# A decode layer's forward and backward pass: dP rows turned by VectorE, dq four heads at a time, rows spread by one product, P of pairs by two groups, wq as 32-bit words

## The chip, the cores and the metric

The kernel runs on one core of a Trainium2 chip, in one launch. The metric is the time of one execution on the device in microseconds (us); the time before is the median of three runs. Engines are named as in the profile: PE is TensorE, DVE VectorE, ACT ScalarE, POOL GpSimd, and SP the engine whose queue issues nearly all DMA transfers, in order.

## The reference, cut to what matters

One decode step (one query row per batch element) of a pre-layernorm attention block with a cached K and V, followed by a gated MLP, and the gradients with respect to all inputs. B = 4, H = 32 heads (128 batch-heads in all), 4096 cached positions, head size 128, width 512, F = 1792, all bfloat16.

```python
def _A_ref(x, k_cache, v_cache, wq, wo):
    q = (x @ wq).reshape(B, Sq, H, Dh) ...
    scores = jnp.einsum("bhqd,bhkd->bhqk", q, k_cache) * (Dh ** -0.5)
    p = _softmax(scores, axis=-1)
    o = jnp.einsum("bhqk,bhkd->bhqd", p, v_cache)
    return (...o...).reshape(B, Sq, H * Dh) @ wo
x = A_x
h = x + _A_ref(_layernorm(x), A_k_cache, A_v_cache, A_wq, A_wo)
h2 = h + _B_ref(_layernorm(h), B_w1, B_w3, B_w2)
...
_out, _vjp = jax.vjp(_f, A_x, A_k_cache, A_v_cache, A_wq, A_wo, B_w1, B_w3, B_w2)
_grads = _vjp(grad_out)
```

For each batch-head, with one query row, the gradient of V is the outer product of P (4096) and dO (128), and the gradient of K the outer product of dS (4096) and q (128). dS = P * (dP - c), with dP = V dO and c = sum(P * dP). K and V are 1 MB for each batch-head (128 MB each), and so are their gradients: 128 MB of K read once, 128 MB of V read twice, and two gradients of 128 MB written.

## The kernel before, in words

The kernel is built with an explicit order: instructions stand on each engine in the order in which the Python code calls them. Semaphore waits are put in where a tile or a slot is reused.

SBUF holds an arena of 23 slots of 1 MB (`Slot`; two neighbours make a `Slot2`). In the first part of the gradient stage a slot is taken from the head of a list of free slots (`free`), and `give`/`gave` appends it at the end. Taking a slot is decided when the program is built. Whoever writes into it at run time waits until its last users are done: PE for a V slot, the landing of the store for a gradient slot.

The work goes in four stages.
1. Up to about 655 us: for each batch-head, K is transposed, scores, softmax and P are computed, and M = V^T (P K), a 128x128 matrix, is kept in f32 (it holds o, and dq is computed from it). The weights are loaded at the end of it.
2. The middle, to about 700 us: attention output, layernorm, MLP forward and backward, and dh. At its end the first two dV products (`grad_V(0)`, `grad_V(1)`) are made, whose slots are kept in `first_gv`, and V of batch-heads 0 to 8 has been asked for (`load_V2`).
3. Batch-heads 0 to 31 one by one (`SP = 32`): `front(s)` transposes V as 32-bit words (four groups: PE transposes, ACT copies back, `words_T`, L792 to L799) and multiplies it by dO. Eight matmuls (L1245) add a head's dP into one PSUM tile of four heads, through the windows `zd` that POOL fills (`dO_window`, L1211). Then the V slot is given back (L1249 to L1253). `rows_out` (ACT, L1221) and `rows_T` (PE, L1228) turn the rows, `group_dS` (DVE, L1261, L1264) makes dS for four heads. `grad_V(s)` and `grad_K(s)` make the outer products on DVE (`outer`, L813) and store them (L824, L1271). P is doubled for `outer` by POOL (`P_pairs`, L1216); the rows of dO and q are spread to all partitions four heads at a time by `replicate` (PE, L1186, ACT, L1189).
4. Batch-heads 32 to 127 as 48 pairs, 2 MB each: `front_pair`, `group_dS_pair`, `grad_pair` (products L1400, stores L1410), `P_rows` and `replicate_pair` do the same for two heads.

Beside stages 3 and 4 run three generators, a step at a time (`side`): "o" (the rest of dO; `dO_rows`), "q" (`dq_work`: one matmul by M for each batch-head, L1007) and, from s = 35, "s" (dx, the weights' gradients and the second output).

The order in which stage 3 begins is the caller's loop (L = 5, `more_V` calls `grad_V`):

```python
for s in range(L):
    load_ahead(s)
    front(s)
    if s == 0:
        for gv in first_gv:
            gv.give()
    more_V((4, 6, 7, 8, 9)[s])
```

`load_ahead` issues the next V load once `front` has put a V slot into `vring`. A V slot goes there only when fewer than seven V slots are held; the first two go to `free`.

Of the kernel before, what the change touches and what calls it, by code (L numbers as in the profile page):

```python
# [21 lines left out]
SP = 32  # L22
# [5 lines left out]
def kernel(  # L28
# [133 lines left out]
    rows_t = pers.tile([32 + B, D], FP32, name="rows_t")  # L162
# [638 lines left out]
    def words_of(v, g, k):  # L801
        return v.rearrange("p (x r t) -> p t x r", r=Dh, t=2)[:, k, 4 * g:4 * g + 4]
# [40 lines left out]
    with ExitStack() as cm:  # L843
# [77 lines left out]
        dh = rs.f(2080)[0:B, 1024:1024 + D]  # L921
# [50 lines left out]
    with ExitStack() as c2:  # L972
        psT = c2.enter_context(tc.tile_pool(name="psT2", bufs=2, space=bass.MemoryType.PSUM))
        psD = c2.enter_context(tc.tile_pool(name="psD", bufs=1, space=bass.MemoryType.PSUM))
# [29 lines left out]

        def dq_work():
            for s in range(NH):
                nc.tensor.matmul(dq_ps[:, s:s + 1], lhsT=M_of(s)[:, 0:Dh], rhs=dOT_f[:, s:s + 1], start=True, stop=True)  # L1007
                if s % MC == MC - 1:
                    Ms[s // MC].give()
                    if s // MC in (5, 6):  # L1010
                        load_wq2(s // MC - 5)
                if s % 4 == 3:
                    yield
# [3 lines left out]
        def side_work():  # L1017
# [4 lines left out]
            t = rs.f(2080)[:, 1536:1536 + NH]  # L1022
            nc.vector.tensor_tensor(out=t, in0=c_rep[:], in1=kPT[:], op=ALU.mult)
            nc.vector.tensor_tensor(out=t, in0=dq_ps[:, 0:NH], in1=t, op=ALU.subtract)
# [6 lines left out]
            nc.scalar.copy(out=dqr_bf[:], in_=pt[:])  # L1031
            flat = Slot("dqflat")
# [7 lines left out]
            for cc in range(DC):  # L1040
                wq2 = wq2s.popleft()
                wv = wq2.b(HD).rearrange("p (n c) -> p n c", c=P)
                for h0 in range(0, H, 8):
                    pt = psg.tile([P, 8, P], BF16, tag="gps", name="pt_wq")
                    for i in range(8):
                        nc.tensor.transpose(pt[:, i, :], wv[:, h0 + i, :], ident_b[:])
                    yield
                    nc.scalar.copy(out=wv[:, h0:h0 + 8, :], in_=pt[:])
                yield
                for h in range(H):  # L1050
                    nc.tensor.matmul(dx_ps[0:B, cc * P:(cc + 1) * P], lhsT=dqT_bf[:, h * B:(h + 1) * B], rhs=wv[:, h, :],
                                     start=(h == 0), stop=(h == H - 1))
                    if h == H // 2 - 1:
                        yield
                wq2.give()
                load_wq2(cc + 2)
                yield
# [10 lines left out]
            nc.vector.tensor_tensor(out=dx_bf, in0=dh, in1=lnbx, op=ALU.add)  # L1068
# [22 lines left out]
            nc.gpsimd.tensor_copy(out=dh_bf, in_=dh)  # L1091
# [71 lines left out]
        def rest_of_dO():  # L1163
            for pg in range(1, H // 8):
# [6 lines left out]
                mid_w["wo"][pg].give()  # L1171
                yield
# [5 lines left out]
        units["o"] = rest_of_dO()  # L1178
        def replicate(nm_, i0):
# [3 lines left out]
            rows = dOrows_bf if nm_ == "rdo" else qrows_bf  # L1183
            ps = psrep.tile([P, REP, Dh], FP32, tag="rep", name="rep_ps")
            for i in range(REP):
                nc.tensor.matmul(ps[:, i, :], lhsT=ident_b[0:K_, i0 + i:i0 + i + 1].to_broadcast([K_, P]), rhs=rows[0:K_, :],  # L1186
                                 start=True, stop=True)
# [7 lines left out]
        dOw = bw3.tile([P, 2, SP], BF16, name="dOw", tag="dOw", bufs=1)  # L1195
        for i in range(B):
            nc.gpsimd.memset(zd[i][:], 0.0)
# [20 lines left out]
        def rows_out():  # L1218
            if "ps" in rows:
                rows["sb"] = bw3.tile([P, 512], FP32, tag="dPr", name="dPr", bufs=1)  # L1220
                nc.scalar.copy(out=rows["sb"][:], in_=rows.pop("ps")[:])  # L1221

        def rows_T():
            if "sb" in rows:
                sb = rows["t"] = rows.pop("sb")
                rows["T"] = psD.tile([P, B, P], FP32, tag="dPT", name="dPT_ps")
                for jj in range(4):
                    nc.tensor.transpose(rows["T"][:, jj, :], sb[:, jj * P:(jj + 1) * P], ident_f[:])  # L1228

        def front(s):  # L1230
            hl = s % B
            if s not in VTs:
                for g in range(SJ // GW):
                    V_T(s, psT, range(g, g + 1))
                    if hl == 0 and g == 0:
                        rows_out()
                    if hl == 0 and g == 2:
                        rows_T()
            v = VTs[s].t[:, 0:SJ * Dh]
            if hl == 0:  # L1240
                rows["acc"] = psD.tile([P, 512], FP32, tag="dP", name="dP_ps")
            dO_window(s + 2)
            for k in range(2):
                for c in range(4):
                    nc.tensor.matmul(rows["acc"][32 * c:32 * (c + 1), :], lhsT=zd[hl][:, k, :], rhs=words_of(v, c, k),  # L1245
                                     start=(hl == 0 and k == 0), stop=(hl == B - 1 and k == 1), tile_position=(0, 32 * c))
            if hl == B - 1:
                rows["ps"] = rows.pop("acc")
            sl = VTs.pop(s)  # L1249
            if nv["next"] < SP and len(V2s) + len(VTs) + len(vring) < NV2:  # L1250
# [296 lines left out]
```

## Time and profile before

| what | value |
|---|---|
| time, median of 3 runs | 1688.53 us (1688.17 to 1689.38) |
| the profiled execution's own time | 1688.41 us |
| its span, first to last instruction | 1686.6 us |
| PE / DVE / ACT / POOL busy | 75% / 73% / 57% / 23% of the span |
| bytes moved by DMA | 707.21 MB, mean 419 GB/s |
| mean granted PE clock | 0.855 |
| largest waits | DVE L1400 for the landing of stores, 260.1 us; POOL L453 for ACT, 409.5 us; SP's queue for DVE L1400, 559.8 us |

A busy share is a mean over stages. The page cuts the span into 40 slices of 42 us: a digit is the busy share of a slice in tenths, and the GB/s row is what the transfers moved. A line of a group or of the timeline has the line of the code, the engine, the operation, what it writes and reads with shapes, and in brackets how long the engine stood idle before it and what ended that. A wait is put down to the last of several semaphores.

### The profile page before, as it was taken

What the parts mean: (1) busy time and instruction counts of PE and PEld (TensorE: products, weight loads), DVE (VectorE), ACT (ScalarE), POOL (GpSimd) and SP (SyncE); (2) the same over time, 40 slices, a digit from 0 to 9 for tenths busy, and PEclk for the clock granted to TensorE, in tenths of its full rate; (3) what the DMA queues carried; (4) which work ended last, traced back from release to release, by engine and by line L of the source; (5) the groups of instructions that cost most, each with busy time, mean ns of one, the idle gap of its engine ahead of it and who ended that gap; (6) DMA issues with size and microseconds to landing.
All of it is one profiled execution on the core that took longest, in us unless ns stands there. A gap on an engine that the chain in (4) does not pass through costs nothing.

```text
span 1686.6 us, 33967 instructions
## 1 busy us (share of the span) xinstructions
PE 1260.6 (75%) x14188; PEld 924.3 (55%) x14188; DVE 1233.9 (73%) x1198; ACT 960.9 (57%) x1492; POOL 379.6 (23%) x663
## 2 busy tenths in 40 slices
PE   5989888888888888878878666667766677776660
PEld 4777777677667766745555544544434444444440
DVE  5999899989998997667766476576565656555673
ACT  3455454445445454677666556666655676666650
POOL 1221222222232222234541131111120101011020
PEclk9999999999999999799899778777678676567775
DMA  9999999999999999999999999999999999999996
GB/s 400 424 424 424 425 423 425 424 424 421 418 423 411 424 411 397 398 410 426 425 426 428 429 429 429 431 430 429 429 430 430 429 429 431 430 429 431 430 429 259
DMA packets 80986, 707.21 MB, mean 419 GB/s; under 512 B 8748, under 2 KB 12984, under 8 KB 15296
## 3 DMA queue, kind: packets, MB, share of 16 engines
q1 hardware_dynamic: 80416, 704.94, 99.2%
q8 instruction: 112, 1.84, 0.4%
q14 instruction: 42, 0.34, 0.0%
q0 software_dynamic: 416, 0.10, 0.0%
HBM read 422.59 MB, written 282.34 MB: 418 GB/s over the span
## 4 chain that ended last, share of the span: by engine, by line
DMA 35%; DVE 7%; ACT 5%; PE 5%; issue 3%; DVEq 0%; SPq 0%; POOL 0%; ACTq 0%
DMA out_dram<-arena 34%; DVE arena L1400 7%; ACT arena L799 5%; PE pt_tps L798 1%; PE dq_ps L1007 1%; PE dP_ps L1245 1%; DMA arena<-in_A_v_cache_dram 1%; PE pt_wo L610 0%; DVEq L1542 0%; PE rep_ps L1186 0%; DVE dPr L1342 0%; ACT dPr L1221 0%; PE dOT_ps L773 0%; PE dPT_ps L1228 0%; PE c_ps L784 0%
## 5 line engine op out<-in xcount | busy, mean ns | idle before, releaser
L799 ACT COPY arena<-pt_tps 128x1024 bf16<-128x1024 bf16 x512 | 491.7, 1023 | 249.0 <-PE pt_tps L798 247.3
L798 PE MATMUL pt_tps<-ident_f,arena 128*128 128x128 f32 x2048 | 410.7, 356 | 202.9 <-DMA arena<-in_A_v_cache_dram 125.6
L798 PEld LDWEIGHTS pt_tps<-ident_f,arena 128*128 128x128 f32 x2048 | 304.1, 182 | 349.3 <-issue 191.6
L1400 DVE TENSOR_TENSOR arena<-arena 128x8192 bf16<-128x8192 bf16 x48 | 212.5, 4427 | 197.9 <-DMA out_dram<-arena 192.5
L457 DVE TENSOR_TENSOR arena<-arena 128x4096 bf16<-128x4096 bf16 x128 | 292.4, 2285 | 24.0 <-POOL arena L453 24.0
L472 PE MATMUL M_ps<-arena 128*128 128x130 bf16 x4096 | 286.9, 223 | 30.0 <-DMA arena<-in_A_v_cache_dram 29.2
L472 PEld LDWEIGHTS <-arena 128*128 128x128 bf16 x4096 | 254.6, 99 | 49.6 <-DMA arena<-in_A_v_cache_dram 42.5
L1400 DVE TENSOR_TENSOR arena<-dS,arena 128x8192 bf16<-128x8192 bf16 x48 | 212.3, 4424 | 67.6 <-DMA out_dram<-arena 67.6
L364 DVE STREAM_TRANSPOSE arena<-arena 128x512 f32<-128x512 f32 (+1 forms) x321 | 250.6, 797 | 0.0
L359 ACT COPY arena<-pt_tps 128x1024 bf16<-128x1024 bf16 x128 | 129.4, 1012 | 180.4 <-PE pt_tps L358 149.6
L1397 POOL COPY arena<-arena 128x128 bf16<-128x128 bf16 x48 | 43.7, 912 | 432.7 <-ACT arena L1374 200.0
L370 POOL TENSOR_TENSOR W<-qrep,wmask 128x128 bf16<-128x128 bf16 x128 | 120.8, 944 | 85.4 <-PE S_ps L390 70.6
L453 POOL COPY arena<-P_all 128x64 bf16<-128x64 bf16 x128 | 32.7, 256 | 412.5 <-ACT P_all L447 409.5
L1308 POOL COPY arena<-arena 64x4 bf16<-64x4 bf16 x96 | 68.8, 717 | 136.3 <-PE dP_ps L1328 108.6
L1328 PE MATMUL dP_ps<-arena 128*32 128x512 bf16 x768 | 84.4, 471 | 8.4 <-ACT arena L799 8.3
L813 DVE TENSOR_TENSOR arena<-dS,arena 128x4096 bf16<-128x4096 bf16 x32 | 73.1, 2291 | 21.8 <-DMA out_dram<-arena 21.5
L447 ACT COPY P_all<-pt_P 32x64 bf16<-32x64 bf16 x256 | 52.1, 203 | 54.1 <-PE pt_P L443 51.8
L358 PE MATMUL pt_tps<-ident_b,arena 128*128 128x128 bf16 x1024 | 80.8, 224 | 0.0
L482 PE MATMUL kP_ps<-arena,onesw 128*32 128x512 bf16 x1024 | 79.4, 387 | 0.0
L813 DVE TENSOR_TENSOR arena<-P,arena 128x4096 bf16<-128x4096 bf16 x29 | 66.3, 2291 | 17.7 <-DMA out_dram<-arena 17.5
L422 ACT ACTIVATE E<-S_ps,nm 128x256 f32<-128x256 f32 x64 | 30.4, 474 | 82.7 <-DVE nm L419 82.6
L991 PE MATMUL gps<-arena 4*128 4x512 bf16 x110 | 47.3, 452 | 39.0 <-ACT arena L985 39.0
(246 smaller groups left out, 1494.7 us busy)
## 6 DMA issues: line engine op xcount, KB each, us to landing
out_dram<-arena SPq DMA_DIRECT2D x96, 2048.0 KB, 27.4
arena<-in_A_v_cache_dram SPq DMA_DIRECT2D x160, 1024.0 KB, 15.6
arena<-in_A_k_cache_dram SPq DMA_DIRECT2D x128, 1024.0 KB, 15.4
arena<-in_A_v_cache_dram SPq DMA_DIRECT2D x48, 2048.0 KB, 31.7
out_dram<-arena SPq DMA_DIRECT2D x72, 1024.0 KB, 19.8
arena<-in_A_wq_dram SPq DMA_DIRECT2D x8, 1024.0 KB, 14.3
arena<-in_B_w_dram SPq DMA_DIRECT2D x8, 896.0 KB, 15.0
out_dram<-arena SPq DMA_DIRECT2D x6, 896.0 KB, 27.6
```

Of the source, the lines that this page charges most:

```text
L358: nc.tensor.transpose(pt[:, i, :], Kn[:, c * GW + i, :], ident_b[:])
L359: nc.scalar.copy(out=KT[:, c * GW:(c + 1) * GW, :], in_=pt[:])
L364: nc.vector.transpose(out=KT[:, c * w_:(c + n) * w_], in_=Kn[:, c * w_:(c + n) * w_])
L370: nc.gpsimd.tensor_tensor(out=W[:, hl], in0=qrep[:, :, s:s + 1].to_broadcast([P, 4, 32]), in1=wmask[:, hl, None, :].to_broadcast([P, 4, 32 ...
L457: nc.vector.tensor_tensor(out=PK[:, :, 0:Dh].rearrange("p j (r t) -> p j r t", t=2), in0=Ks[s].heads().rearrange("p j (r t) -> p j r t", t=2),
L472: nc.tensor.matmul(hold["M"][:], lhsT=Vn[:, j, :], rhs=PK[:, j, :], start=(j == 0), stop=(j == SJ - 1))
L482: nc.tensor.matmul(hold["kP"][32 * q:32 * (q + 1), :, :], lhsT=ones_window(w), rhs=PK[:, j0:j0 + 4, 0:Dh], start=(w == 0 and c == 0), stop ...
L798: nc.tensor.transpose(ptw[:, jj, :], w[:, 4 * g + jj, :], ident_f[:])
L799: nc.scalar.copy(out=v.rearrange("p (j d) -> p j d", d=Dh)[:, g * GW:(g + 1) * GW, :], in_=pt[:])
L813: nc.vector.tensor_tensor(out=dst.rearrange("p j (r t) -> p j r t", t=2), in0=col2[:, :, None, :].to_broadcast([P, SJ, Dh // 2, 2]), in1=r ...
L1328: nc.tensor.matmul(rows["acc"][32 * c:32 * (c + 1), :], lhsT=zt[t % B][:, k, ZP - m:ZP - m + 32], rhs=words_of(v, 2 * c + u, k), start=(pl ...
L1400: nc.vector.tensor_tensor(out=dst.rearrange("p (j r t) -> p j r t", r=Dh // 2, t=2), in0=col2[:, :, None, :].to_broadcast([P, 2 * SJ, Dh / ...
```

## The change

Six parts, by what they do:
- The dP rows of a group, in PSUM, are turned by one VectorE transpose of 32x32 blocks (`rows_turned`) in place of a ScalarE copy and four PE transposes. `words_of` takes other columns so that the blocks land where they are wanted, and the windows of the pairs (`zt`) are laid out anew.
- `front` no longer multiplies at its end: it puts the head into `pend`, and `products()` makes its matmuls and gives the slot back, in the middle of the next `front` (at g = 2), or after `side` in the main loop.
- dq is computed for four heads by one f32 matmul of 512 columns against a window of four dO columns (`dz`, filled by POOL); the wanted diagonal is taken out at the end of the generator (`m4f`) and turned once.
- Rows of dO and q are spread by one POOL product each (`spread`, with a mask `m4`), so that `replicate` is one matmul of 512 columns in place of four of 128; `replicate_pair` likewise two in place of eight.
- P of pairs (`P_rows`) is made for two groups by four matmuls.
- wq is transposed as 32-bit words: 64 f32 transposes in place of 128, with dq's words split to match (`dqw`). `dh` moves to `rows_t`.

```diff
-        dh = rs.f(2080)[0:B, 1024:1024 + D]
+        dh = rows_t[64:64 + B, :]
+        RM = {nm_: rs.t[:, 2048 + 512 * k:2560 + 512 * k].rearrange("p (i d) -> p i d", i=REP) for k, nm_ in enumerate(("rq", "rdo"))}
...
-        psD = c2.enter_context(tc.tile_pool(name="psD", bufs=1, space=bass.MemoryType.PSUM))
+        psD = c2.enter_context(tc.tile_pool(name="psD", bufs=2, space=bass.MemoryType.PSUM))
...
+        dz = rs.t[:, 4032:4152].bitcast(FP32)
+        nc.gpsimd.memset(dz, 0.0)
+
         def dq_work():
-            for s in range(NH):
-                nc.tensor.matmul(dq_ps[:, s:s + 1], lhsT=M_of(s)[:, 0:Dh], rhs=dOT_f[:, s:s + 1], start=True, stop=True)
-                if s % MC == MC - 1:
+            for s in range(0, NH, 4):
+                nc.gpsimd.tensor_copy(out=dz[:, 28:32], in_=dOT_f[:, s:s + 4])
+                yield
+                g, c = s % 32 // 4, s // 32
+                Mv = Ms[s // MC].f(MC * (Dh + 1)).rearrange("p (n c) -> p n c", c=Dh + 1)[:, s % MC:s % MC + 4, 0:Dh]
+                nc.tensor.matmul(dq_ps[32 * c:32 * (c + 1), :], lhsT=dz[:, 28 - 4 * g:60 - 4 * g], rhs=Mv, start=(g == 0), stop=(g == 7),
+                                 tile_position=(0, 32 * c))
+                if s % MC == MC - 4:
                     Ms[s // MC].give()
                     if s // MC in (5, 6):
                         load_wq2(s // MC - 5)
-                if s % 4 == 3:
-                    yield
+            yield
 
...
-                    pt = psg.tile([P, 8, P], BF16, tag="gps", name="pt_wq")
-                    for i in range(8):
-                        nc.tensor.transpose(pt[:, i, :], wv[:, h0 + i, :], ident_b[:])
+                    pt = psg.tile([P, 4, P], FP32, tag="gps", name="pt_wq")
+                    for i in range(4):
+                        nc.tensor.transpose(pt[:, i, :], ww[:, h0 // 2 + i, :], ident_f[:])
                     yield
-                    nc.scalar.copy(out=wv[:, h0:h0 + 8, :], in_=pt[:])
+                    nc.scalar.copy(out=wv[:, h0:h0 + 8, :].rearrange("p n c -> p (n c)"),
+                                   in_=pt.rearrange("p n c -> p (n c)").bitcast(BF16))
...
+                if pg == H // 8 - 1:
+                    spread("rdo", P)
...
+        def spread(nm_, n):
+            rws = dOrows_bf if nm_ == "rdo" else qrows_bf
+            nc.gpsimd.tensor_tensor(out=RM[nm_][0:n], in0=rws[0:n, None, :].to_broadcast([n, REP, Dh]),
+                                    in1=m4[0:n, :, None].to_broadcast([n, REP, Dh]), op=ALU.mult)
+
+        spread("rdo", 8 * B)
+        spread("rq", P)
...
             ps = psrep.tile([P, REP, Dh], FP32, tag="rep", name="rep_ps")
-            for i in range(REP):
-                nc.tensor.matmul(ps[:, i, :], lhsT=ident_b[0:K_, i0 + i:i0 + i + 1].to_broadcast([K_, P]), rhs=rows[0:K_, :],
-                                 start=True, stop=True)
+            nc.tensor.matmul(ps[:], lhsT=s4[0:K_, i0 // REP:i0 // REP + 1].to_broadcast([K_, P]), rhs=RM[nm_][0:K_],
+                             start=True, stop=True)
...
-        def rows_out():
-            if "ps" in rows:
-                rows["sb"] = bw3.tile([P, 512], FP32, tag="dPr", name="dPr", bufs=1)
-                nc.scalar.copy(out=rows["sb"][:], in_=rows.pop("ps")[:])
-
-        def rows_T():
-            if "sb" in rows:
-                sb = rows["t"] = rows.pop("sb")
-                rows["T"] = psD.tile([P, B, P], FP32, tag="dPT", name="dPT_ps")
-                for jj in range(4):
-                    nc.tensor.transpose(rows["T"][:, jj, :], sb[:, jj * P:(jj + 1) * P], ident_f[:])
+        pend = []
 
         def front(s):
-            hl = s % B
             if s not in VTs:
                 for g in range(SJ // GW):
+                    if g == 2:
+                        products()
                     V_T(s, psT, range(g, g + 1))
-                    if hl == 0 and g == 0:
-                        rows_out()
-                    if hl == 0 and g == 2:
-                        rows_T()
-            v = VTs[s].t[:, 0:SJ * Dh]
-            if hl == 0:
-                rows["acc"] = psD.tile([P, 512], FP32, tag="dP", name="dP_ps")
             dO_window(s + 2)
-            for k in range(2):
-                for c in range(4):
-                    nc.tensor.matmul(rows["acc"][32 * c:32 * (c + 1), :], lhsT=zd[hl][:, k, :], rhs=words_of(v, c, k),
-                                     start=(hl == 0 and k == 0), stop=(hl == B - 1 and k == 1), tile_position=(0, 32 * c))
-            if hl == B - 1:
-                rows["ps"] = rows.pop("acc")
-            sl = VTs.pop(s)
-            if nv["next"] < SP and len(V2s) + len(VTs) + len(vring) < NV2:
-                vring.append(sl.i)
-            else:
-                gave(sl.i, stored=False)
+            products()
+            pend.append(s)
+
+        def products():
+            for s in pend:
+                hl = s % B
+                v = VTs[s].t[:, 0:SJ * Dh]
+                if hl == 0:
+                    rows["acc"] = psD.tile([P, 512], FP32, tag="dP", name="dP_ps")
+                for k in range(2):
+                    for c in range(4):
+                        nc.tensor.matmul(rows["acc"][32 * c:32 * (c + 1), :], lhsT=zd[hl][:, k, :], rhs=words_of(v, 0, c, k),
+                                         start=(hl == 0 and k == 0), stop=(hl == B - 1 and k == 1), tile_position=(0, 32 * c))
+                if hl == B - 1:
+                    rows["ps"] = rows.pop("acc")
+                sl = VTs.pop(s)
+                if nv["next"] < SP and len(V2s) + len(VTs) + len(vring) < NV2:
+                    vring.append(sl.i)
+                else:
+                    gave(sl.i, stored=False)
+            pend.clear()
+
+        def rows_turned():
+            r = bw3.tile([P, 512], FP32, tag="dPr", name="dPr", bufs=1)
+            nc.vector.transpose(out=r[:], in_=rows.pop("ps")[:])
+            return r.rearrange("p (x m) -> p x m", m=32)
 
...
             i0 = g * B
-            T = rows.pop("T").rearrange("p jj (c m) -> p c jj m", c=4)
-            t = rows.pop("t")[:, 0:B * SJ].rearrange("p (b j) -> p b j", b=B)
-            t5 = t.rearrange("p b (c jj i) -> p b c jj i", c=4, i=2)
+            R = rows_turned()
+            t = dSt.rearrange("p (b j) -> p b j", b=B)
+            t4 = t.rearrange("p b (x i) -> p b x i", i=2)
             for hl in range(B):
-                nc.vector.tensor_scalar(out=t5[:, hl], in0=T[:, :, :, 2 * hl:2 * hl + 2], scalar1=c_rep[:, i0 + hl:i0 + hl + 1],
+                nc.vector.tensor_scalar(out=t4[:, hl], in0=R[:, :, 2 * hl:2 * hl + 2], scalar1=c_rep[:, i0 + hl:i0 + hl + 1],
                                         scalar2=scale, op0=ALU.subtract, op1=ALU.mult)
...
-            Pp[q] = True
-            ps = psrep.tile([P, B, 2, SJ], FP32, tag="rep", name="Pp_ps")
-            s = SP + q * 2 * B
+            Pp[q] = Pp[q + 1] = True
+            ps = psrep.tile([P, 2 * B, 2, SJ], FP32, tag="rep", name="Pp_ps")
+            v = P_all[:, SP + q * 2 * B:SP + (q + 2) * 2 * B, :].rearrange("p (q a l) j -> p a q (l j)", q=2, a=2)
             for a in range(2):
                 for par in range(2):
-                    nc.tensor.matmul(ps[64 * a:64 * (a + 1), :, par, :], lhsT=ident_b[:, par:P:2],
-                                     rhs=P_all[:, s + a * B:s + (a + 1) * B, :], start=True, stop=True, tile_position=(0, 64 * a))
-            nc.scalar.copy(out=Pp["s"].b(NT * 2 * SJ)[:, q * B * 2 * SJ:(q + 1) * B * 2 * SJ],
+                    nc.tensor.matmul(ps[64 * a:64 * (a + 1), :, par, :], lhsT=ident_b[:, par:P:2], rhs=v[:, a], start=True,
+                                     stop=True, tile_position=(0, 64 * a))
+            nc.scalar.copy(out=Pp["s"].b(NT * 2 * SJ)[:, q * B * 2 * SJ:(q + 2) * B * 2 * SJ],
...
-            rws = dOrows_bf if nm_ == "rdo" else qrows_bf
             ps = psrep.tile([P, REP, Dh], FP32, tag="rep", name="rep_ps")
-            for i in range(REP):
-                for a in range(2):
-                    n = s + i + a * B
-                    nc.tensor.matmul(ps[64 * a:64 * (a + 1), i, :], lhsT=ident_b[0:K_, n:n + 1].to_broadcast([K_, P // 2]),
-                                     rhs=rws[0:K_, :], start=True, stop=True, tile_position=(0, 64 * a))
+            for a in range(2):
+                n = s // REP + a
+                nc.tensor.matmul(ps[64 * a:64 * (a + 1)], lhsT=s4[0:K_, n:n + 1].to_broadcast([K_, P // 2]),
+                                 rhs=RM[nm_][0:K_], start=True, stop=True, tile_position=(0, 64 * a))
...
             if s == 0:
                 replicate("rdo", REP)
+        products()
         group_dS(0)
...
             side(s)
+            products()
```

## The prediction, made before the changed kernel was run

> **What bounds the kernel now.** I read the page's 40 slices first: where is any engine full, and does the transfer rate follow it?
>
> ```profile
> PE   5989888888888888878878666667766677776660
> DVE  5999899989998997667766476576565656555673
> ...
> DMA  9999999999999999999999999999999999999996
> GB/s 400 424 424 424 425 423 425 424 424 421 418 423 411 424 411 397 398 410 426 425 426 428 429 429 429 431 430 429 429 430 430 429 429 431 430 429 431 430 429 259
> ...
> q1 hardware_dynamic: 80416, 704.94, 99.2%
> ```
>
> The reader should see that the DMA row is full in every slice but the last, while PE and DVE fall to 5 to 7 tenths from slice 18 on. The kernel moves 707.2 MB at a rate that does not depend on them. So cheaper compute is worth nothing in itself; only a stretch in which the transfers starve, or are given work later, moves the end. The rate dips in slices 15 to 17 (397, 398, 410), which is where the change begins. Next I read that stretch in windows of 5 us (columns: busy us and count of each engine, granted clock, DMA share, GB/s):
>
> ```profile
> 700.00:705.00 5.00, 2.80 (x21) 1.66 (x21) 3.00 (x3) 1.81 (x4) 4.67 (x15) 0.63 1.00 405
> 705.00:710.00 5.00, 4.18 (x22) 2.36 (x21) 3.87 (x3) 3.85 (x4) 1.49 (x3) 0.69 0.70 293
> 710.00:715.00 5.00, 3.50 (x25) 1.90 (x26) 4.72 (x3) 3.76 (x4) 3.07 (x4) 1.00 1.01 421
> 715.00:720.00 5.00, 3.55 (x28) 2.19 (x28) 5.00 (x3) 4.35 (x5) 4.94 (x3) 1.00 1.03 393
> 720.00:725.00 5.00, 3.89 (x28) 2.30 (x24) 2.60 (x7) 3.91 (x5) 2.24 (x7) 1.00 0.95 316
> ...
> 1100.00:1400.00 300.00, 204.39 (x1217) 128.64 (x1217) 187.61 (x102) 191.81 (x243) 45.56 (x64) 0.73 1.01 430
> ```
>
> At 705 to 710 the DMA share is 0.70: the only place after the start where transfers run dry. The timeline of VectorE shows why; these are the first products P x dO of `grad_V`, 1 MB each:
>
> ```profile
> 696.79 2.29 DVE L813 TENSOR_TENSOR arena<-arena 128x4096 bf16<-128x4096 bf16 x1
> ...
> 703.71 2.31 DVE L813 TENSOR_TENSOR arena<-arena 128x4096 bf16<-128x4096 bf16 x1 [2.00 <-POOL zd L1211]
> 706.94 2.29 DVE L813 TENSOR_TENSOR arena<-P,arena 128x4096 bf16<-128x4096 bf16 x1 [0.93 <-DMA out_dram<-arena]
> 709.44 2.31 DVE L813 TENSOR_TENSOR arena<-P,arena 128x4096 bf16<-128x4096 bf16 x1 [0.20 <-DMA out_dram<-arena]
> 711.92 9.17 DVE L813 TENSOR_TENSOR arena<-P,arena 128x4096 bf16<-128x4096 bf16 x4 [0.17 <-DMA out_dram<-arena]
> ```
>
> The V loads queued earlier are through by 704.4 (landing records of the trace), and until 717 nothing but these products feeds the queue. From the 4th on each begins as an earlier one's store lands and frees its slot. Issues on SP are at 699.11, 701.63, 706.04, 709.26, 711.78, 714.24, 716.67; the stores issued at 709.26, 711.78 and 714.24 land 4.97, 4.89 and 4.88 us later. So a slot's round trip is 2.30 (product) + 4.90 + about 0.13 = 7.3 us. Three slots give 1 MB each 2.4 us, just what the queue moves (1.05 MB at 430 GB/s: 2.44 us).
>
> **The part that sets the sum: when the first V slot comes free.** Before, `front(0)` ends with the dP products and returns head 0's slot; the list of free slots is then that slot and the two of `first_gv`, and the 3rd product takes it. After, `front(0)` only appends to `pend`; `products()` returns the slot inside `front(1)`, behind `more_V(4)`, so the 3rd product takes the first one's slot. The built order of both kernels says the same: before, the 3rd waits for the dP matmuls and the 4th to 7th for the store three places back; after, the 3rd to 6th wait for the store two places back, the 7th takes head 0's slot, the 8th and 9th reach three and four places back. All later waits on stores reach back five or more places in both. Two slots give 1 MB each 3.65 us. Step by step, after:
> - 3rd: starts when the 1st has landed (706.9, as the 4th does before), issued 709.26, alone in the queue, lands 714.2. Before: issued 706.04.
> - 4th: 2nd landed 709.35, product 709.45 to 711.75, lands 716.7.
> - 5th: 714.3 to 716.6, lands 721.5. 6th: 716.8 to 719.1, lands 724.0. Before, the 6th (issued 714.24) landed at 719.12.
>
> The 6th store is 4.9 us late. Behind it SP's queue holds in both the 7th, 8th and 9th stores and the loads of V heads 9, 10 and 11 (one load moves behind the 8th store, one behind the 9th); in-order, they are late too, but from there the queue has more than it can move, so nothing is added. Before, these six took 719.12 to 736.63 = 17.5 us for 6 x 2.44 = 14.6: 2.9 us were lost where reads rejoin the writes (393 and 316 GB/s in the windows above). If that loss is bound to the rejoining, it recurs and the whole 4.9 stays; if it was chance, 2.0 stays. Bounds 2.0 and 4.9; the trace has one such rejoining and it was slow, so I take two thirds of it: +3.9.
>
> The Trainium skill, DMA: Bandwidth & Descriptors, section on the anatomy of one DMA, gives 2.0 us plus bytes at 436 GB/s for a transfer (a fit on GpSimd's path), an estimate of 4.4 us for 1 MB. By it the two-slot chain would bring the 6th store to 723.0 and the sum 1.0 us lower; the measured 4.9 is of these very stores and decides.
>
> **The other edits,** all costed at nothing because the queue is full meanwhile (share 1.01 at 1100 to 1400) and VectorE idles 265 us waiting for stores before L1400 (197.9 + 67.6):
> - dP rows: gone are 32 ScalarE copies (L1221, 592 ns: 18.9 us), 128 PE passes (L1228, 28.6 us) and 64- and 32-wide scalings; added are 32 VectorE transposes of 128x512 f32 out of PSUM. Nearest row: L364, 667 ns at least from SBUF, 1242 for twice the width; I take 0.7, 22 us in all. Scaling of pairs halves (96 x 283 ns to 48). VectorE gains about 9 us over 950 us. Without the cover it would be 0.3 us a group. PE no longer waits 0.53 us for ScalarE before a head's last dP products.
> - `spread`: one GpSimd product of 128x512 replaces weights of single columns. Bounds from L370 (128x128, 407 ns median) and L951 (128x16, 221): slope 1.66 ns a column, 1.05 us; at most 4 x 0.407. Two stand ahead of the zd and P copies at the start: after c_rep and two small reduces, 702.0 to 704.1, then memsets and zd (1.3 us), then P of heads 3 to 5 at about 706.2 instead of 703.5. The 4th product starts at 709.45, so 3 us spare. PE's four `rep` matmuls become one of 512 columns (128x512 in L1245: 398 ns against 4 x 214).
> - dq: 256 PE records (34.2 us) become 32 f32 products of 512 columns; from L1328's 0.47 us, two to four times: 30 to 60 us, on a PE busy 68 to 80%. Each waits for a GpSimd copy made one `side` step earlier, which stands behind P copies that wait for VectorE; behind that matmul PE holds the next head's transposes, but those wait on a load that SP issues behind the same products.
> - P by two groups, wq by words (128 transposes to 64), the longer dqT path (about 2 us of VectorE), `dh` moved, a 4.5 us GpSimd cast (L1091) to VectorE: off the path, covered likewise.
> - 493 of 13,910 built matmuls go, with as many weight loads: 64 KB at 65 bytes each (q8 moves 1.84 MB for PE's 28,376 records), 4 of its 112 packets. A packet occupies one of 16 engines about 1 us: 0.2 us in all.
>
> Sum: 1688.4 (profiled execution; span 1686.6 and 1.8 around it; the median of runs is 1688.53) + 3.9 - 0.2 = 1692.1; I say **1692.2 us**.
>
> **Rivals.**
> - *The rejoining costs nothing this time.* 1688.4 + 2.0 - 0.2 = 1690.2. For: packets are slow there, 428 ns against 309, only for 5 us, and reads and writes mix later at 424 to 430 GB/s. Against: it is the one time that a first read meets a run of stores.
> - *Not slower: the pause is taken out of the tail.* From 1660 to 1687 us the DMA share is 0.37: by the packet records one of 16 engines ends 12 us after the next. If a pause at 710 to 720 lets the lagging engine draw level, the end stays: 1688.3. It decides if that lag exists by 710. Against: landings spread 1.1 us at 719 and 2.5 at 731; the lag grows after 900, so only 1 to 2 us can be absorbed.
> - *A deeper stall on GpSimd.* A GpSimd copy that meets an outer product waits it out: zd copies take 183 ns at least, 2294 at most. If the spreads take 3.8 us each (four times L370's mean of 944), P of head 3 is ready at 711.5, the 4th and 6th product slip 2.0 us; a further 2.3 if one meets the 3rd product. 1694.2 to 1696.5.
>
> **How the numbers follow.** Chances: forecast 0.56, fast rejoining 0.26, tail 0.08, deeper stall 0.10. The forecast's own range is 1691.1 (landings of 4.4 us) to 1693.3 (the loss in full). For 8 in 10: 1689.0, between tail and fast rejoining, to 1695.6, within the deeper stall. 0.2% is 3.4 us, about what a measurement can tell here: slower means over 1691.9. That takes nearly all of the deeper stall and most of the forecast, with the upper end of the others: 0.62; within 0.33; faster 0.05, since no stretch has 3.4 us to give but the tail.
>
> **What would show it.** In the profile after: the 3rd `grad_V` product starts near 707, not 703.7, with "DMA out_dram<-arena" before it, and the 5th near 714; DMA share under 0.7 twice between 705 and 718; the first L840 on SP after the stores near 724; the same 429 to 431 GB/s from slice 22 on. Wrong if the 3rd product keeps its place, if the share after 900 differs, or if the last engine's lag changes by more than 2 us.

## The result, and the profile after

| | before | after |
|---|---|---|
| median of 5 runs each, us (lowest to highest) | 1688.53 (1687.46 to 1689.38) | 1702.53 (1701.77 to 1703.99) |
| profiled execution, us (span) | 1688.41 (1686.6) | 1703.0 (1700.8) |
| bytes moved, MB (mean GB/s over the span) | 707.21 (419) | 707.14 (416) |

After over before is 1.0084, 95% interval 1.007 to 1.0098: 14.0 us slower, where 3.7 us had been forecast and 1695.6 us was the upper end of the range. The same bytes take longer, so the question is where the queue ran slower or dry. The rows of the page of the changed kernel that answer to the first fence of the prediction:

```profile
PE   5889888888888888975774556557666676676650
...
DVE  5989899899899987577776666586565656555683
...
DMA  9999999999999999999999999999999999999996
GB/s 397 418 419 418 419 418 418 419 419 418 411 416 411 418 401 394 374 378 426 425 425 430 428 429 427 430 425 431 430 431 429 428 430 431 430 428 425 430 430 264
...
q1 hardware_dynamic: 80416, 704.94, 99.0%
```

The DMA row is full in every slice but the last, as before. But slices 2 to 10 (counted from 1 here; the prediction counts them from 0) stand at 418 to 419 GB/s, where the kernel before has 421 to 425. These slices are the first stage, which the change does not touch: up to about 690 us both kernels send the same instructions. The second place is the start of the third stage: slices 17 and 18 have 374 and 378 (398 and 410 before). From slice 22 to the last but one the rates are 425 to 431, against 428 to 431.

Now windows. First stage, kernel before, then changed kernel (columns as in the prediction; the last two are DMA share and GB/s):

```profile
0.00:100.00 100.00, 74.94 (x1164) 59.87 (x1165) 77.52 (x123) 44.30 (x87) 21.12 (x67) 0.97 0.99 414
100.00:300.00 200.00, 174.58 (x2926) 143.04 (x2924) 183.67 (x247) 104.06 (x228) 48.99 (x120) 0.99 1.01 424
300.00:500.00 200.00, 169.42 (x2825) 140.03 (x2823) 185.85 (x245) 98.81 (x224) 53.37 (x120) 0.99 1.01 422
```

```profile
0.00:100.00 100.00, 71.98 (x1144) 58.00 (x1145) 76.60 (x122) 44.15 (x87) 21.61 (x67) 0.98 0.99 409
100.00:300.00 200.00, 173.14 (x2907) 142.64 (x2907) 182.13 (x243) 102.29 (x223) 48.75 (x120) 0.99 1.01 419
300.00:500.00 200.00, 171.29 (x2788) 140.50 (x2787) 181.92 (x240) 97.20 (x221) 50.17 (x115) 0.97 1.01 416
```

The share is 1.01 in both: the queue never waits for work, it only moves less while it is full. What is left is the packet. In the first 690 us the loads move in 8 KB packets; by the packet records a packet takes 309 ns in 31,997 of 33,899 cases before and in 5,232 of 33,464 after, where 313 and 311 ns are the commonest; the means are 312.2 and 316.1 ns. That is 1.25%, and 1.25% of 690 us is 8.6 us. The first `grad_V` product starts at 705.00 us instead of 696.79: 8.2 us late before any changed instruction has run.

The start of the third stage in the changed kernel, as VectorE's timeline shows it (start, length, line, count, and in brackets the idle time before and what ended it):

```profile
705.00 2.29 DVE L813 TENSOR_TENSOR arena<-arena 128x4096 bf16<-128x4096 bf16 x1
...
707.53 2.28 DVE L813 TENSOR_TENSOR arena<-arena 128x4096 bf16<-128x4096 bf16 x1
...
715.29 2.29 DVE L813 TENSOR_TENSOR arena<-arena 128x4096 bf16<-128x4096 bf16 x1 [4.99 <-DMA out_dram<-arena]
717.77 2.29 DVE L813 TENSOR_TENSOR arena<-P,arena 128x4096 bf16<-128x4096 bf16 x1 [0.18 <-DMA out_dram<-arena]
721.67 2.29 DVE L813 TENSOR_TENSOR arena<-P,arena 128x4096 bf16<-128x4096 bf16 x1 [1.61 <-ACT arena L799]
724.71 4.49 DVE L813 TENSOR_TENSOR arena<-P,arena 128x4096 bf16<-128x4096 bf16 x2 [0.75 <-POOL zd L1257]
730.46 2.29 DVE L813 TENSOR_TENSOR arena<-P,arena 128x4096 bf16<-128x4096 bf16 x1 [1.26 <-DMA out_dram<-arena]
...
735.19 0.70 DVE L1297 STREAM_TRANSPOSE dPr<-dP_ps 128x512 f32<-128x512 f32 x1
```

The third product begins 10.3 us after the first (6.9 before) and waits 4.99 us for the first one's store: this is the step that the prediction rests on. The windows there:

```profile
705.00:710.00 5.00, 4.53 (x55) 3.97 (x53) 4.96 (x6) 2.58 (x6) 0.66 (x2) 0.50 1.01 408
710.00:715.00 5.00, 3.67 (x19) 2.09 (x20) 0.30 (x2) 2.71 (x4) 4.34 (x17) 0.50 0.82 336
715.00:720.00 5.00, 4.45 (x31) 2.98 (x30) 4.52 (x2) 4.08 (x5) 0.00 (x0) 0.83 0.43 182
720.00:725.00 5.00, 3.92 (x30) 2.08 (x28) 2.64 (x3) 5.00 (x7) 0.78 (x4) 1.00 0.77 315
725.00:730.00 5.00, 3.38 (x32) 1.90 (x32) 4.20 (x2) 4.52 (x5) 2.75 (x5) 1.00 0.90 362
1100.00:1400.00 300.00, 200.69 (x1123) 122.80 (x1122) 185.07 (x93) 189.55 (x229) 43.90 (x60) 0.69 1.01 429
```

The queue starves from 710 to 725, down to a share of 0.43. To put a number to it, count landings from the first store of `gv` on: the 12 transfers from that store to the load of V head 11 end 29.78 us after the store's landing in the kernel before and 33.74 us after it in the changed one. So of the 14.2 us between the two spans, 8.35 are there when the first store lands, 3.96 come in the next 11 landings, and 1.9 in the 950 us behind them.

### The profile page after: what moved, and what is told of

Same layout as the page of the kernel before. It is cut to its first block, busy times and chain, and to the rows that moved or that the text cites. A ratio compares the mean times of both kernels' runs of the same rounds, so it can differ in the third digit from the quotient of the medians.

```text
span 1700.8 us, 33039 instructions
## 1 busy us (share of the span) xinstructions
PE 1222.9 (72%) x13599; PEld 864.1 (51%) x13599; DVE 1241.6 (73%) x1191; ACT 942.5 (55%) x1456; POOL 398.3 (23%) x700
## 2 busy tenths in 40 slices
DMA packets 80982, 707.14 MB, mean 416 GB/s; under 512 B 8748, under 2 KB 12984, under 8 KB 15296
## 4 chain that ended last, share of the span: by engine, by line
DMA 44%; DVE 9%; PE 4%; ACT 2%; issue 2%; DVEq 0%; POOL 0%; SPq 0%; ACTq 0%; POOLq 0%
DMA out_dram<-arena 40%; DVE arena L1436 6%; DMA arena<-in_A_v_cache_dram 4%; DVE arena L813 1%; ACT arena L799 1%; PE M_ps L472 1%; DVE arena L457 1%; PE pt_w L601 0%; PE pt_tps L798 0%; PE dq_ps L1015 0%; PE dP_ps L1284 0%; ACT Pn L436 0%; PE pt_wo L610 0%; DVEq L1581 0%; PE kP_ps L482 0%
## 5 line engine op out<-in xcount | busy, mean ns | idle before, releaser
L798 PEld LDWEIGHTS pt_tps<-ident_f,arena 128*128 128x128 f32 x2048 | 300.6, 181 | 398.5 <-issue 223.9
L472 PEld LDWEIGHTS <-arena 128*128 128x128 bf16 x4096 | 254.7, 100 | 75.3 <-DMA arena<-in_A_v_cache_dram 69.5
L1353 POOL COPY arena<-arena 64x4 bf16<-64x4 bf16 x96 | 96.7, 1007 | 152.3 <-PE dP_ps L1368 148.7
L1433 POOL COPY arena<-arena 128x128 bf16<-128x128 bf16 x48 | 35.1, 732 | 371.7 <-DVE arena L1436 245.3
L1368 PE MATMUL dP_ps<-arena 128*32 128x512 bf16 x768 | 75.1, 473 | 20.4 <-ACT arena L799 19.7
L358 PEld LDWEIGHTS <-arena 128*128 128x128 bf16 x1024 | 62.9, 100 | 25.9 <-issue 25.8
```

Of the source, the lines that this page charges most:

```text
L358: nc.tensor.transpose(pt[:, i, :], Kn[:, c * GW + i, :], ident_b[:])
L472: nc.tensor.matmul(hold["M"][:], lhsT=Vn[:, j, :], rhs=PK[:, j, :], start=(j == 0), stop=(j == SJ - 1))
L798: nc.tensor.transpose(ptw[:, jj, :], w[:, 4 * g + jj, :], ident_f[:])
L1353: nc.gpsimd.tensor_copy(out=zt[t % B][r_, :, :, ZP + 4 * (t % 2) + i], in_=zt[B][r_, :, s - SP:s2 - SP + 1:B])
```

## The experiments

**Where the first 8 us come from.** In the diff one line adds bytes to what lies ahead of the arena in each partition: `m4f`, 16 bytes per partition, is taken from the pool `small` (`rows_t` in `pers` gets more partitions, but no more bytes in each). The pools stand in the order const, pers, small, slotp (the arena). As both programs are built, the arena begins at byte 30336 of each partition before and at 30368 after: 30336 is 237 x 128, 30368 lies 32 bytes above that: the 16 bytes take up 32. A slot is 8320 bytes, 65 x 128, so all slots share the base's distance from a multiple of 128. Theory A: this alone slows the loads. Rival: something else in the changed kernel, or the run. Two runs from both sides: the changed kernel with the tile elsewhere, and the kernel before with a tile that only takes room.

```diff
-            m4f = small.tile([P, REP], FP32, tag="m4f", name="m4f", bufs=1)
+            m4f = bw3.tile([P, REP], FP32, tag="m4f", name="m4f", bufs=1)
```

> The changed kernel with its 16-byte tile m4f taken from pool bw3, which lies behind the arena, instead of small, which lies ahead of it: the arena begins at byte 30336 of each partition again, as in the kernel before, and not at 30368. Theory A (the first 690 us, whose instructions are the same in both kernels, read at 418-419 GB/s instead of 424 because every load now lands 32 bytes off a multiple of 64): 8 KB packets go back to 309 ns, slices 2 to 10 to 424 GB/s, the first grad_V product from 705.0 back to about 696.8 us, and the time to 1692.5 us (1702.5 less 8.2 in the first stage and less up to 1.9 later). Rival B (the lower rate belongs to the placing of something else, or to the run): 1702.5 us, first product at 705.

Measured: 1693.59 us (1692.54 to 1696.42), 1.0032 of the kernel before, interval 1.002 to 1.0043. First product at 697.38 us; the window of the first stage is back at the rate before:

```profile
100.00:300.00 200.00, 175.51 (x2929) 143.44 (x2926) 184.00 (x247) 104.46 (x228) 48.46 (x120) 0.99 1.01 424
```

8.9 us (1702.53 - 1693.59) come back by moving 16 bytes. The median is 1.1 us above the 1692.5 expected; its six runs begin at 1692.54. Then the other side, on the kernel before (n is 32, 64, 96, 128):

```diff
         dq_ps = psx.tile([P, 512], FP32, tag="x2", name="dq_ps")
+        pad_ = small.tile([P, n // 4], FP32, tag="pad_", name="pad_", bufs=1)
+        nc.gpsimd.memset(pad_[:], 0.0)
```

> The kernel before with nothing but a tile of 32 bytes per partition added to pool small and cleared once by GpSimd: the arena begins at byte 30368, as in the changed kernel. Theory A (the arena's address alone sets the lower rate): first grad_V product at about 705 instead of 696.8 us and 1697 to 1699 us in all. Rival B (something else in the changed kernel): 1688.5 us.

> As the run with 32 bytes, but with 64: the arena begins at 30400, a multiple of 64 though not of 128 (30336 is a multiple of 128). If what matters is a multiple of 64: 424 GB/s, packets of 309 ns and 1688.5 us. If it is a multiple of 128: 418 GB/s or less and 1697 us or more. If any larger base costs: as the run with 32 bytes.

> The kernel before with a tile of 128 bytes per partition added to pool small and cleared by GpSimd as in the runs with 32 and 64: the arena begins at 30464, again a multiple of 128. If a multiple of 128 is what matters: 424 GB/s in the first stage, packets of 309 ns, 1688.5 us. If any larger base, or the added tile and its clearing, costs: 1698 us as with 32 and 64.

> As before, with 96 bytes: the arena begins at 30432, 96 off a multiple of 128. If a multiple of 128 is what matters, 1698 us as with 32 and 64 off; if the cost grows with the distance from a multiple of 128: 1701 us or more.

| kernel | arena at | over a multiple of 128 | 8 KB packets of the first 690 us: mean ns | at 309 ns | median, us | ratio to before |
|---|---|---|---|---|---|---|
| before | 30336 | 0 | 312.2 | 94% | 1688.5 | |
| before, 32 bytes | 30368 | 32 | 316.2 | 15% | 1698.13 | 1.0043 to 1.0068 |
| before, 64 bytes | 30400 | 64 | 315.9 | 17% | 1698.32 | 1.0043 to 1.0071 |
| before, 96 bytes | 30432 | 96 | 316.4 | 18% | 1699.01 | 1.0047 to 1.0072 |
| before, 128 bytes | 30464 | 0 | 311.9 | 97% | 1686.76 | 0.9979 to 0.9997 |

The windows of the runs with 32 and with 128 bytes (with 32 the first product begins at 703.88 us, where 705 had been expected):

```profile
100.00:300.00 200.00, 174.12 (x2906) 143.33 (x2906) 182.07 (x243) 102.43 (x223) 48.71 (x120) 0.98 1.01 419
```

```profile
100.00:300.00 200.00, 176.01 (x2937) 143.25 (x2934) 184.27 (x247) 104.56 (x228) 48.28 (x120) 0.99 1.01 424
```

So the address alone costs 9.4 us (1698.13 - 1688.76, the kernel before on the same chip), much the same at 32, 64 and 96 bytes (the 1701 us of a cost that grows did not come), and nothing at a multiple of 128. That a larger base or the added clearing costs is out: 128 bytes have both and are not slower. The two profiled executions differ by 9.8 us; 8.1 of these are there when the first store lands (714.92 against 706.85) and the rest comes later: from that landing to the last transfer it takes 980.2 us against 978.5. The run with 128 bytes is 1.8 us faster than the kernel before; in its profiled execution the first store lands 2.2 us earlier. The cause of that was not tested.

**What the 4 us at the start of stage 3 consist of.** Theory A: the products of head 0, sent in `front(1)`, give its V slot back too late for the third `grad_V` product. Rival: the queue makes the pause up. First this step undone alone in the changed kernel, with the arena still at 30368:

```diff
             pend.append(s)
+            if s == 0:
+                products()
```

> The changed kernel with the products of head 0 sent at the end of front(0), so that its V slot is given back before more_V(4) as in the kernel before; the arena stays at 30368. Theory A (the deferred products cost 4.0 us at the start of the third stage, by the delay of the store and V landings there, and the address the rest): third grad_V product not held up by the first store, the lag of the landing of V11 behind the kernel before down from 12.3 to about 8.3 us, 1698.5 us in all. Rival B (the pause is taken up later by the queue, so that the start does not count): 1702.5 us.

Measured: 1699.99 us (1697.57 to 1700.42): 2.5 us come back, not 4.0, and the eleventh landing is at 32.26 us after the first store's, between 29.78 and 33.74. The median lies between the two expectations. Theory A's 1698.5 us is still inside the interval (1697.2 to 1701.6 us), so the time alone does not decide; but the landing does not come back to that of the kernel before, so a part was missing. PE's timeline names it. These are the products of head 0 in the kernel before, and in the changed kernel with this edit:

```profile
702.45 1.04 PE L1245 MATMUL dP_ps<-arena,zd 128*32 128x512 bf16 x8 [1.28 <-POOL zd L1211]
```

```profile
714.02 1.05 PE L1286 MATMUL dP_ps<-arena,zd 128*32 128x512 bf16 x8 [3.69 <-POOL zd L1257]
```

They wait for the head's window `zd` on GpSimd, 3.69 us instead of 1.28. GpSimd's own timeline of the second kernel:

```profile
709.18 1.68 POOL L786 CAST dOT_f<-dOT_bf 128x32 f32<-128x32 bf16 x1 [4.34 <-PE c_ps L784]
...
711.21 1.03 POOL L1220 TENSOR_TENSOR arena<-dOrows_bf,m 32x512 bf16<-32x512 bf16 x1 [0.28 <-issue]
712.21 1.03 POOL L1220 TENSOR_TENSOR arena<-qrows_bf,m 128x512 bf16<-128x512 bf16 x1
713.19 0.40 POOL L1243 MEMSET zd<- 128x64 bf16 x4
713.54 0.91 POOL L1257 COPY zd<-dOw 64x2 bf16<-64x2 bf16 x4
```

The two spreads (L1220, 1.03 us each) stand ahead of the windows (L1257). So the slot is held back twice: by the order of PE's work, and by GpSimd's when PE's order is mended. Now with the arena at 30336 throughout, a table of two by two. The spreads are sent later by this edit:

```diff
-        spread("rdo", 8 * B)
-        spread("rq", P)
...
         for s in range(2):
             dO_window(s)
+        spread("rdo", 8 * B)
         for s in range(3, 6):
             P_pairs(s)
+        spread("rq", P)
```

> The changed kernel with m4f moved (arena at 30336) and, besides, the products of head 0 sent at the end of front(0). Theory A (address and slot add up; of the 4.8 us that m4f moved still loses, the slot is 1.5 to 2.5, as the pair 1702.5 and 1700.0 showed with the arena at 30368, because the products of head 0 now stand behind the two spreads on GpSimd): 1691 to 1692 us, the eleventh landing after the first store at 32.3 us against 29.8 in the kernel before and 33.3 with m4f moved alone. Rival B (the slot is the whole of the rest): 1688.8 us.

> The changed kernel with m4f moved and the two spreads (1.03 us each on GpSimd) sent behind the first two head windows zd, the second of them behind P of heads 3 to 5 too; the products of head 0 stay in front(1). Theory A (while the products of head 0 are deferred the slot comes back late anyway, so the spreads hide behind that): 1693 to 1693.6 us, as with m4f moved alone. Rival B (the spreads alone hold the slot back): 1691 us or less.

> All three: m4f moved, the products of head 0 at the end of front(0), and the spreads behind the windows. Theory A (three causes, nothing else: the products wait for zd some 1.3 us, as in the kernel before, instead of 3.7, and V slot 0 comes back 6.9 us after the first grad_V product instead of 9.3): eleventh landing at 29.8 us, 1688.3 to 1689.0 us, the time before. Rival B (a part of the rest comes from the later loop, where all products are deferred and GpSimd copies more): 1690 us or more.

| median, us (ratio to before, interval) | spreads ahead of the windows | spreads behind |
|---|---|---|
| head 0's products in `front(1)` | 1693.59 (1.002 to 1.0043) | 1692.88 (1.0016 to 1.0037) |
| head 0's products in `front(0)` | 1690.43 (1.0001 to 1.0019) | 1689.36 (0.9996 to 1.0014) |

Down the columns the order on PE is worth 3.2 and 3.5 us, along the rows the spreads 0.7 and 1.1; both of these lie within the spread of the runs. (The first cell was measured beside a kernel before of 1688.76 us, the other three beside one of 1688.59.) With both mended and the arena in its old place the changed kernel takes the time of the kernel before, to within its interval. The first of the three came out between its two expectations, the other two near theory A, the last 0.4 us above it.

The landings of the profiled executions bear this out in one column only. With the spreads behind, the eleventh landing goes from 34.13 us after the first store's to 30.02 when head 0's products are sent early. With the spreads ahead it goes from 33.27 to 33.82, where 32.3 had been expected, and the third product, still held by `zd`, begins 9.3 us after the first (9.6 with the products in `front(1)`):

```profile
708.34 2.31 DVE L813 TENSOR_TENSOR arena<-arena 128x4096 bf16<-128x4096 bf16 x1 [4.02 <-POOL zd L1257]
```

That execution, of 1692.06 us, is the slowest of its ten. So the 3.2 us of the left column are measured in time, but where they are won is not shown.

VectorE in the run with both mended:

```profile
696.75 2.29 DVE L813 TENSOR_TENSOR arena<-arena 128x4096 bf16<-128x4096 bf16 x1
...
699.28 2.28 DVE L813 TENSOR_TENSOR arena<-arena 128x4096 bf16<-128x4096 bf16 x1
...
703.75 3.00 DVE L813 TENSOR_TENSOR arena<-arena 128x4096 bf16<-128x4096 bf16 x1 [1.70 <-DMA arena<-in_A_v_cache_dram]
707.22 4.78 DVE L813 TENSOR_TENSOR arena<-P,arena 128x4096 bf16<-128x4096 bf16 x2 [0.47 <-DMA out_dram<-arena]
```

The third product begins 7.0 us after the first, for 6.9 before (the bracket names a V load, but what came last is the end of head 0's products on PE, at 703.5). It also lasts 3.00 us instead of 2.29, and on GpSimd the second spread takes 3.13 us where the first took 1.03:

```profile
702.99 1.03 POOL L1220 TENSOR_TENSOR arena<-dOrows_bf,m 32x512 bf16<-32x512 bf16 x1
703.97 0.57 POOL L1260 COPY P<-P_all 128x64 bf16<-128x64 bf16 x3
704.51 3.13 POOL L1220 TENSOR_TENSOR arena<-qrows_bf,m 128x512 bf16<-128x512 bf16 x1
```

The two engines met twice: when the product was sent at 703.75, GpSimd was busy with the first spread and the copies until 704.54, and the second spread, sent at 704.51, ended 0.9 us after the product.

The same step put into the kernel before, by itself:

```diff
+            if s > 0:
+                products(s)
+            else:
+                pend.append(s)
...
                 for g in range(SJ // GW):
+                    if g == 2 and pend:
+                        products(pend.pop())
                     V_T(s, psT, range(g, g + 1))
```

> The kernel before with one thing altered: the eight products of head 0 are sent in the middle of front(1) instead of at the end of front(0), so that its V slot comes back after the sixth grad_V product has been asked for. The term of the prediction by itself: the third grad_V product waits for the first store (2.0 + 3.3 us instead of 2.0), eleventh landing at 33 to 34 us instead of 29.8, and 1692.0 to 1692.7 us. Rival B (the pause is taken up again): 1688.8 us.

Measured: 1694.34 us, but only four runs and far apart (1691.95 to 1697.88); the interval is 1.0026 to 1.006. The third product waits 3.03 us for the first store, and the eleventh landing is at 32.84 us:

```profile
706.69 2.29 DVE L813 TENSOR_TENSOR arena<-arena 128x4096 bf16<-128x4096 bf16 x1 [3.03 <-DMA out_dram<-arena]
```

The sign and the mechanism hold. The median, 5.8 us over the kernel before, lies above the 1692.0 to 1692.7 us expected, and the cause of that is open; with four runs the size is less certain than in the table.

**A version that is faster than both.** The last run keeps the whole change, with head 0's products in `front(0)`, the spreads behind, and `m4f` in `small` with 128 bytes, the base at which the kernel before was 1.8 us faster:

```diff
-            m4f = small.tile([P, REP], FP32, tag="m4f", name="m4f", bufs=1)
+            m4f = small.tile([P, 32], FP32, tag="m4f", name="m4f", bufs=1)[:, 0:REP]
```

> The changed kernel with the products of head 0 at the end of front(0), the spreads behind the windows, and m4f left in small but with 128 bytes, so that the arena begins at 30464, where the kernel before ran in 1686.8 us. If that base is better by itself: 1687.5 us (1689.4 less 1.8), as fast as the kernel before or faster. If the 1.8 us belong to the kernel before alone: 1689.4 us.

Measured: 1687.01 us (1685.58 to 1688.66), 0.9989 of the kernel before, interval 0.998 to 0.9998. It is faster than both, by 0.11% against the kernel before; the kernel before with 128 bytes, 1686.76, is as fast. The gain goes with the base: 2.3 us against the same edits at 30336 (1689.36), for 1.8 in the kernel before. Its profiled execution (1688.66 us) has the eleventh landing at 33.01 us after the first store's, where the same edits at 30336 had 30.02, with the third product 7.0 us after the first in both: a landing figure of one execution can be off by 3 us.

## Why the prediction was wrong, point by point

- **The queue as the bound: right.** Share 1.01 in the full stretches of both kernels, 429 GB/s at 1100 to 1400 against 430. By the packet records the last DMA engine ends 14.2 us behind the median engine in both, so the tail took up nothing.
- **The sum: here it failed.** "1688.4 + 3.9 - 0.2" takes all 690 us ahead of the change as unchanged, since their instructions are. They were not: the step that is missing is the place of the buffers. `m4f` moves the arena by 32 bytes, at 9.4 us by itself (kernel before with 32 bytes). The diff named the pool, and the sum had no term for it: the address was put at nothing without a reason. With the arena back in its place (`m4f` moved), the changed kernel takes 1693.59 us, within the 8-in-10 range of 1689.0 to 1695.6 and 1.4 us above the forecast, though just above the forecast's own upper bound, given as 1693.3 (1688.4 + 4.9 - 0.2 is 1693.1).
- **The V slot: right in mechanism, near in size.** Forecast +3.9. Measured: 3.96 by the landings of one execution each, the spreads included; 3.2 and 3.5 us by the table; 5.8, loosely, in the kernel before. Measured from the first product's start, the third was forecast at 10.1 us and began at 10.3, the fifth 17.5 and 16.7, the sixth 20.0 and 19.7; the sixth store landed at 27.8, against 27.2 forecast. Three details were off. The share fell below 0.7 once (0.43, in windows of 5 us), not twice; later waits ended on ScalarE and GpSimd as well, but that this is why is not shown. The third store, alone in the queue, took 3.93 us from issue to landing, not the 4.9 of the prediction. And the sixth store was 5.3 us late (17.59 against 12.26 us after the first), not 4.9, of which the rejoining gave back 1.4 by V head 11, where 1.0 had been taken. The two misses cancel: that 3.96 falls on 3.9 is in part luck.
- **The spreads: price right, place wrong.** Estimated at 1.05 us, measured 1.03. But "3 us spare" was reckoned to P of head 3. The windows `zd` stand behind them too, and the fence of the prediction shows the third product of the kernel before already waiting "2.00 <-POOL zd L1211": no spare there. By the table the spreads cost 0.7 us with the deferred products and 1.1 without, neither clear of the spread of the runs; the wait for `zd`, 3.69 us for 1.28, is what shows them.
- **The other edits at nothing: right.** The transposes took 708 ns, 22.6 us in all, for 22 forecast:

```profile
L1297 DVE STREAM_TRANSPOSE dPr<-dP_ps 128x512 f32<-128x512 f32 x32 | 22.6, 708 | 0.0
```

With all of them in and the three causes out, the time is 1689.36 us, 1.0005 of before (0.9996 to 1.0014), so together they are worth at most 2.4 us. The 0.2 us for less PE code can't be told from nothing.
- **The rivals.** Fast rejoining, 1690.2, and the tail, 1688.3, did not come; nor did the deeper stall as described: the spreads that stood ahead kept to 1.03 us. Slower was the likeliest outcome forecast, by 3.7 us; it came true, but two thirds of the 14.0 us came from a cause that the forecast did not have. Without the address it would have been 4.8.

The causes add up: 9.4 (kernel before with 32 bytes) and 4.8 (changed kernel with `m4f` moved, 1693.59 - 1688.76) make 14.2, for 14.0 measured. By the table, 3.5 of the 4.8 are the deferred products, 0.7 the spreads, and the 0.8 that stay with all three undone (1689.36 - 1688.59) can't be told from nothing.

## What to carry to other kernels

Before costing a change by its instructions, compare where the buffers lie in both programs: a small tile in a pool ahead of a large one moves everything behind it, and on a kernel bound by loads that can outweigh the rest. Look first at a stage that the change does not touch: if its rate differs at the same full DMA share, the cause is not in the instructions. And when a buffer is given back by one engine, ask for every engine in the chain that leads to it what is newly queued ahead, not only for the engine whose order was changed.

## What the runs showed of the hardware

- In the first stage, which only loads, transfers into SBUF with an 8 KB run per partition ran at 424 GB/s (100 to 300 us) with bases at multiples of 128 bytes and at 419 with bases 32, 64 or 96 bytes off, the DMA share full in both (packets of 312 against 316 ns on the mean). The Trainium skill, Collectives: The Full Stack, section on rules for kernel authors, asks for the buffers of collectives to be aligned to 32 bytes; no run here has a collective, and for these plain loads 32 was not enough. DMA: Bandwidth & Descriptors of the same skill, section on how a descriptor splits into AXI transactions, speaks of starts at multiples of 256 bytes; here 128 was enough, since slots of 65 x 128 bytes lie by turns on a multiple of 256 and 128 off one, and 94% of the packets took 309 ns (97% with the base at 30464).
- Between 740 and 900 us, where loads and stores mix, the same displaced arena costs next to nothing: 94% of the 8 KB packets of the changed kernel take 309 ns there (96% before), at 425 GB/s against 426. The cause of that was not tested.
- A spread that met an outer product on VectorE took 3.13 us instead of 1.03, and the product 3.00 instead of 2.29, alike in both runs with the spreads behind and head 0's products early. The Trainium skill, SBUF — State Buffer, section on terms, has the two engines share a pair of ports that one instruction holds to its end; this agrees with the trace as far as it goes: the 2.1 us added to the spread are close to the 2.2 that the product still had to run, and the 0.7 added to the product are about what GpSimd's copies still had to run (703.75 to 704.54).
